# An unused room of 128 bytes a partition ahead of x, in a kernel of block attention and a squared-relu FFN

## The chip, the cores and the metric

One core of one Trainium2 chip. The metric is the device time of one execution in microseconds (us). The kernel before takes 895.19 us, the median of three runs (894.81 to 895.62).

## The reference

Attention inside chunks of 64 tokens, then a feed-forward network whose hidden values are `relu(h)` squared. All inputs and outputs are float32.

```python
def _attn_ref(q, k, v):                      # 8 batches, 8 heads, 576 tokens, 64 wide
    ...                                      # q_c, k_c, v_c: nine chunks of 64 tokens
    scores = scale * np.matmul(q_c, k_c.transpose(0, 1, 2, 4, 3))
    scores = scores - np.max(scores, axis=-1, keepdims=True)
    attn = np.exp(scores)
    attn = attn / (np.sum(attn, axis=-1, keepdims=True) + 1e-09)
    out = np.matmul(attn, v_c)
    ...
def _moe_ref(x, w_in, w_out):                # x 4608 x 512, w_in 512 x 2048, w_out 2048 x 512
    h = x @ w_in
    r = np.maximum(h, 0.0)
    g = r * r
    return (g @ w_out)
```

The weights come as 64-bit floats, and the kernel turns them into pairs of 32-bit floats itself.

## The kernel before, in words

The 4608 tokens are 36 pairs of chunks (128 tokens each), and four pairs make one of nine blocks of 512 tokens. For each block the attention writes x, transposed and as a sum of a high and a low part (tiles `xh`, `xl`, lines 338 to 342). The weights stand in SBUF all the time, converted once, each 128 x 512 piece as a high and a low part (`w`, line 176; sixteen rooms of 8192 bytes a partition, two pieces in each).

The FFN of a block has 16 steps f. A step has twelve matmuls of line 509 (`h` = weights x x: the stationary operand is a 128 x 128 slice of `w`, the moving operand 512 columns of `xh` or `xl`), then, two steps later, twelve of line 546 (`o` = g x weights: the stationary operand is a 128 x 128 slice of `gh` or `gl`, the moving operand 512 columns of `w`). Each product of two float32 is made of three: high by high, high by low, low by high. Between them ScalarE and VectorE make g of h (relu, square, high part, low part: lines 520, 524 or 526, 533, 536). On TensorE twelve of line 509 alternate with twelve of line 546, through the whole kernel; at four spots of a block this is broken by a group of 64 x 64 matmuls of the attention of the next block (lines 321 and 264). A planner (`Plan`, line 578) sets the order of the work of all engines from written costs; nothing in it knows addresses.

Tiles are taken from pools that lie one behind the other in each partition: `const` (line 84: `ident`, `warm`, and the sixteen rooms of the weights), `att` (line 85: the maxima `nm` and the sums `nz`, two rooms of 32 bytes each), `xp` (line 86: the tiles of x, 4096 bytes each, in which the results `outh` and `outl` stand as well), `gp` (line 87: `g`, `gh`, `gl`, 2048 bytes each, and one of the two rooms `a` of the weights' conversion), `wst` (line 94, the other `a`) and `nat` (line 120: the attention's own tiles). In the program as built, the rooms of the weights begin at addresses whose remainder to 256 is 160, and all tiles of `xp`, `gp`, `wst` and `nat` at addresses with the remainder 32. Slices inside the tiles of x, g and the weights that matmuls read begin at multiples of 512 bytes, so they keep these remainders.

So, in bytes to 256, a matmul of line 509 reads its moving operand at 32 and one of line 546 at 160. While a matmul runs, the weights of the next one are loaded. Inside a run of twelve of line 509 those are slices of `w` (160), inside one of line 546 slices of `gh` or `gl` (32): the two operands that are read at the same time stand 128 bytes apart to 256. At the change from one line to the other, the last matmul of line 509 (moving: x, 32) runs beside the load of `gh` (32), and the last one of line 546 (moving: `w`, 160) beside the load of `w` (160): there the two have the same remainder.

Of the kernel before, what the change touches and what calls it, by code (L numbers as in the profile page):

```python
# [11 lines left out]
F32 = mybir.dt.float32  # L12
# [10 lines left out]
def kernel(  # L23
# [24 lines left out]
    P = 128  # L48
# [34 lines left out]

    const = ctx.enter_context(tc.tile_pool(name="const", bufs=1))
    att = ctx.enter_context(tc.tile_pool(name="att", bufs=1))
    xp = ctx.enter_context(tc.tile_pool(name="xp", bufs=1))
    gp = ctx.enter_context(tc.tile_pool(name="gp", bufs=2))

# [1085 lines left out]
```

## Time and profile before

| | |
|---|---|
| median of three runs | 895.19 us |
| the profiled execution | 895.07 us |
| its span, from the first to the last instruction | 893.3 us |
| TensorE matmuls, busy | 876.3 us (98%) |
| TensorE weight loads, busy | 700.8 us (78%) |
| VectorE, busy | 410.4 us (46%) |
| ScalarE, busy | 341.8 us (38%) |
| GpSimd, busy | 35.2 us (4%) |
| mean granted clock of TensorE | 0.994 |

The times below are microseconds from the start of the span, in that one execution. PE is TensorE's matmuls, PEld its weight loads, DVE VectorE, ACT ScalarE, POOL GpSimd, SP the queue that issues transfers. The duration of one matmul (some 0.39 us) is longer than its distance to the next start (some 0.23 us), since matmuls are pipelined; what counts for the time is the distance of the starts.

### The profile page before, as it was taken

How to read it: one execution, taken by the hardware profiler on the slowest of the kernel's cores; microseconds unless marked ns; L12 is line 12 of the kernel's file. 1: busy time of each engine (PE TensorE's matmuls, PEld its weight loads, DVE VectorE, ACT ScalarE, POOL GpSimd, SP SyncE). 2: the span in 40 equal slices, each digit the busy share in tenths (PEclk: the TensorE clock that was granted, in tenths of full speed). 3: DMA queues.
4: the chain of work that ended last, by engine and by line, in shares of the span. 5: the costliest groups of instructions: out<-in, count | busy, mean ns of one | idle time of the engine just before them, and what ended most of it. 6: DMA issues, size and time to landing. Idle time of an engine off the chain costs nothing.

```text
span 893.3 us, 15034 instructions
## 1 busy us (share of the span) xinstructions
PE 876.3 (98%) x5890; PEld 700.8 (78%) x5890; DVE 410.4 (46%) x646; ACT 341.8 (38%) x568; POOL 35.2 (4%) x38
## 2 busy tenths in 40 slices
PE   6899999999999999999999999999999999999998
PEld 5676777887788888788888888888788887888886
DVE  5998984344444454444444443344434444322111
ACT  4889763332333333323333333223333333323222
POOL 1000000000000000000000000000000000000000
PEclk9899999999999999999999999999999999999999
DMA  9899133232422233222322232223222420001001
GB/s 218 216 293 282 31 84 98 55 74 60 107 60 59 59 85 82 59 55 52 100 55 48 58 102 57 56 57 101 59 61 61 106 48 24 25 1 48 1 1 47
DMA packets 214150, 70.21 MB, mean 79 GB/s; under 512 B 181312, under 2 KB 203840, under 8 KB 214080
## 3 DMA queue, kind: packets, MB, share of 16 engines
q1 hardware_dynamic: 211968, 68.73, 31.8%
q8 instruction: 46, 0.75, 0.3%
q10 hardware_dynamic: 2112, 0.52, 0.3%
q14 instruction: 24, 0.20, 0.1%
HBM read 52.43 MB, written 16.78 MB: 77 GB/s over the span
## 4 chain that ended last, share of the span: by engine, by line
PE 90%; DMA 5%; SPq 3%; DVE 1%; issue 0%; ACT 0%; ACTq 0%
PE o L546 43%; PE h L509 43%; DMA raw<-in_moe_w_out_dram 4%; PE at L321 2%; PE at L264 1%; SPq L222 1%; SPq L136 1%; SPq L230 1%; DMA qk_raw<-in_q_dram 0%; DVE w L189 0%; DMA vd<-in_v_dram 0%; PE qk L387 0%; PE xt L472 0%; SPq L138 0%; DVE raw L154 0%
## 5 line engine op out<-in xcount | busy, mean ns | idle before, releaser
L509 PE MATMUL h<-xh,w 128*128 128x512 f32 x1152 | 394.1, 398 | 1.3 <-DVE w L189 0.8
L546 PE MATMUL o<-w,gh 128*128 128x512 f32 x1152 | 361.9, 395 | 0.0
L509 PEld LDWEIGHTS h<-xh,w 128*128 128x128 f32 x1152 | 216.1, 188 | 54.7 <-DVE w L189 2.0
L546 PEld LDWEIGHTS o<-w,gh 128*128 128x128 f32 x1152 | 215.8, 188 | 51.1
L536 DVE TENSOR_TENSOR gl<-g,gh 128x512 fp32r<-128x512 f32 x144 | 117.5, 816 | 263.8 <-ACT gh L533 263.6
L546 PE MATMUL o<-w,gl 128*128 128x512 f32 x576 | 227.2, 394 | 0.0
L509 PE MATMUL h<-xl,w 128*128 128x512 f32 x576 | 227.0, 394 | 0.0
L520 ACT ACTIVATE g<-h 128x512 f32<-128x512 f32 x144 | 86.4, 600 | 255.6 <-PE h L509 207.2
L533 ACT CAST gh<-g 128x512 fp32r<-128x512 f32 x144 | 89.4, 621 | 184.8 <-PE o L546 184.6
L546 PEld LDWEIGHTS o<-w,gl 128*128 128x128 f32 x576 | 108.1, 188 | 25.9
L509 PEld LDWEIGHTS h<-xl,w 128*128 128x128 f32 x576 | 108.4, 188 | 24.1
L524 DVE TENSOR_TENSOR g<-g 128x512 f32<-128x512 f32 x64 | 44.3, 692 | 100.2 <-ACT g L520 100.0
L291 POOL TENSOR_TENSOR e<-e,z 128x512 f32<-128x512 f32 x28 | 30.3, 1083 | 719.5 <-DVE z L288 357.9
L526 ACT ACTIVATE g<-g 128x512 f32<-128x512 f32 x80 | 50.6, 632 | 2.4
L334 ACT CAST xh<-at 128x256 fp32r<-128x256 f32 x54 | 20.1, 373 | 72.8 <-PE at L264 52.3
L270 DVE TENSOR_REDUCE m<-at 128x8 f32<-128x512 f32 x27 | 18.7, 692 | 47.4 <-ACT xh L334 47.4
L253 DVE STREAM_TRANSPOSE turn<-raw 128x512 f32<-128x512 f32 x56 | 36.9, 690 | 0.1
L276 DVE TENSOR_TENSOR e<-at,m 128x512 f32<-128x512 f32 x27 | 18.6, 689 | 9.2 <-ACT xh L334 9.2
L321 PEld LDWEIGHTS at<-p,vd 64*64 64x64 f32 x864 | 15.1, 134 | 9.9 <-issue 9.5
L154 DVE TENSOR_SCALAR raw<-raw 128x1024 uint16<-128x1024 uint16 x16 | 21.5, 1388 | 1.3 <-ACT raw L150 1.3
L150 ACT ACTIVATE raw<-raw 128x1024 int32<-128x1024 uint32 x16 | 18.5, 1156 | 8.3 <-DMA raw<-in_moe_w_out_dram 5.8
L336 DVE TENSOR_TENSOR xl<-at,xh 128x256 fp32r<-128x256 f32 x54 | 20.4, 392 | 2.6 <-ACT xh L334 2.6
(67 smaller groups left out, 364.7 us busy)
## 6 DMA issues: line engine op xcount, KB each, us to landing
vd<-in_v_dram SPq DMA_DIRECT2D x144, 64.0 KB, 2.7
raw<-in_moe_w_in_dram SPq DMA_DIRECT2D x16, 512.0 KB, 6.5
raw<-in_moe_w_out_dram SPq DMA_DIRECT2D x16, 512.0 KB, 7.4
raw<-in_q_dram SPq DMA_DIRECT2D x224, 32.0 KB, 2.2
raw<-in_k_dram SPq DMA_DIRECT2D x224, 32.0 KB, 2.2
scr<-t SPq DMA_DIRECT2D x28, 256.0 KB, 2.3
p<-scr SPq DMA_DIRECT2D x112, 64.0 KB, 2.0
out_dram<-outh SPq DMA_DIRECT2D x18, 256.0 KB, 2.3
```

Of the source, the lines that this page charges most:

```text
L154: nc.vector.tensor_scalar(half[:, :, :, 1], half[:, :, :, 3], 0x8000, 0x4000, op0=ALU.bitwise_and, op1=ALU.bitwise_or)
L253: nc.vector.transpose(t.rearrange("p h i -> p (h i)"), self.raw[n].rearrange("p h a d -> p (h a d)"))
L291: nc.gpsimd.tensor_tensor(self.e, self.e, self.z.broadcast_to([P, HH, 2, CH]), op=ALU.mult)
L321: nc.tensor.matmul(self.xt[d, s, g, c].rearrange("p (b i) -> p b i", b=IH), vd[slot_of(self.u)][r, 2 * g + a, c], self.p[r, a, :, g, c], s ...
L336: nc.vector.tensor_tensor(x_of("l", b, s)[dst], src, xh.bitcast(F32)[dst], op=ALU.subtract)
L509: nc.tensor.matmul(self.h[:, :self.n], a[:, c], bb[:, c % HP, :self.n], start=c == 0 and i == 0, stop=c == NCC - 1 and i == 2,)
L520: nc.scalar.activation(self.g, self.h[:, :self.n], AF.Relu)
L524: nc.vector.tensor_tensor(self.g, self.g, self.g, op=ALU.mult)
L526: nc.scalar.activation(self.g, self.g, AF.Square)
L533: nc.scalar.copy(self.gh[:, :self.n], self.g)
L536: nc.vector.tensor_tensor(self.gl[:, :self.n], self.g, self.gh.bitcast(F32)[:, :self.n], op=ALU.subtract)
L546: nc.tensor.matmul(acc[b, j], a[:, j * P:(j + 1) * P], bb, start=f == 0 and i == 0, stop=f == NF - 1 and i == 2,)
```

## The change

One tile more in the pool `att`, ahead of all others of that pool: 2 x 16 float32, 128 bytes a partition. No instruction writes or reads it.

```diff
     att = ctx.enter_context(tc.tile_pool(name="att", bufs=1))
+    att.tile([P, 2, 16], F32, name="rest")
     xp = ctx.enter_context(tc.tile_pool(name="xp", bufs=1))
```

With it, everything that lies behind it, `nm` and `nz` and the pools `xp`, `gp`, `wst` and `nat`, moves by 128 bytes. `ident` and the weights stay. The remainder to 256 of x, g and the attention's tiles becomes 160, that of the weights. The remainders to 128 stay all as they were.

## Rows read from the trace of the kernel before

**Rows 1.** The page: engines' busy time (share) xinstructions; TensorE's clock in 40 slices
```profile
PE 876.3 (98%) x5890; PEld 700.8 (78%) x5890; DVE 410.4 (46%) x646; ACT 341.8 (38%) x568; POOL 35.2 (4%) x38
PEclk9899999999999999999999999999999999999999
```
**Rows 2.** Stages: stretch, length, busy time (count) by engine, clock, DMA share, GB/s
```profile
20.00:60.00 40.00, 35.37 (x297) 27.73 (x298) 37.89 (x54) 32.39 (x48) 2.09 (x2) 0.89 0.89 241
60.00:100.00 40.00, 37.43 (x251) 28.43 (x250) 37.58 (x49) 33.62 (x46) 0.00 (x0) 1.00 0.76 210
...
300.00:400.00 100.00, 100.00 (x665) 80.31 (x664) 43.04 (x70) 31.88 (x56) 4.48 (x5) 1.00 0.31 70
...
870.00:893.30 23.30, 19.27 (x84) 15.29 (x82) 2.77 (x4) 7.08 (x12) 0.00 (x0) 0.98 0.12 45
```
**Rows 3.** The same view, 100 to 870 us: line 509 alone, then line 546 alone
```profile
100.00:870.00 770.00, 395.70 (x1572) 292.81 (x1572) 1.00 0.26 60
...
100.00:870.00 770.00, 385.26 (x1565) 293.64 (x1564) 1.00 0.26 60
```
**Rows 4.** The chain that ended last: start, length, what; 437 to 457 us
```profile
437.63 2.80 PE o L546 x12
440.42 2.80 PE h L509 x12
443.22 2.80 PE o L546 x12
446.02 2.80 PE h L509 x12
...
454.41 2.80 PE o L546 x12
```
**Rows 5.** The same view, 800 to 879 us: first and last of 29 runs
```profile
800.19 2.78 PE h L509 x12
...
878.12 2.78 PE h L509 x12
```
**Rows 6.** Timeline, TensorE, the last 36 matmuls: start, length, instruction; first and last
```profile
880.75 0.62 PE L546 MATMUL o<-w,gh 128*128 128x512 f32 x2
...
888.88 0.39 PE L546 MATMUL o<-w,gl 128*128 128x512 f32 x1
```
**Rows 7.** Groups by line, windows around single matmuls, 442.59 to 443.69 us: busy, mean ns
```profile
L509 PE MATMUL h<-xl,w 128*128 128x512 f32 x1 | 0.4, 398 | 0.0
L509 PE MATMUL h<-xh,w 128*128 128x512 f32 x1 | 0.4, 390 | 0.0
L546 PE MATMUL o<-w,gh 128*128 128x512 f32 x1 | 0.4, 395 | 0.0
L546 PE MATMUL o<-w,gh 128*128 128x512 f32 x1 | 0.4, 392 | 0.0
L546 PE MATMUL o<-w,gl 128*128 128x512 f32 x1 | 0.4, 398 | 0.0
```
**Rows 8.** The same view: the matmul of 420.86 us and the weight load beside it
```profile
L546 PE MATMUL o<-w,gh 128*128 128x512 f32 x1 | 0.4, 404 | 0.0
...
L546 PEld LDWEIGHTS o<-w,gh 128*128 128x128 f32 x1 | 0.2, 192 | 0.0
```
**Rows 9.** Groups by line, the whole span: two-input subtractions of VectorE; weight loads
```profile
L189 DVE TENSOR_TENSOR w<-a,w 128x1024 fp32r<-128x1024 f32 x16 | 19.8, 1240 | 3.9 <-ACT w L178 3.9
L524 DVE TENSOR_TENSOR g<-g 128x512 f32<-128x512 f32 x64 | 44.3, 692 | 100.2 <-ACT g L520 100.0
L509 PEld LDWEIGHTS h<-xh,w 128*128 128x128 f32 x1152 | 216.1, 188 | 54.7 <-DVE w L189 2.0 <-ACT w L178 1.0
```
**Rows 10.** Transfers: line, xcount, KB each, us from issue to landing
```profile
p<-scr SPq DMA_DIRECT2D x112, 64.0 KB, 2.0
out_dram<-outh SPq DMA_DIRECT2D x18, 256.0 KB, 2.3
```

## The prediction

> **What bounds the kernel now.** I read the engines' table of the page first, then the stages, then the chain of waits, and last single matmuls. The table shows TensorE's matmuls busy for 98% of the span, while no other engine comes to half of it [rows 1]; the reader is to see one engine that has no idle time to give. The stages show where this holds. From 20 to 100 us TensorE is busy for 35.4 of 40 and 37.4 of 40 us, and VectorE, which converts the weights, for 37.9 and 37.6 of 40: there VectorE, ScalarE and the transfers of the weights set the pace. From 100 us on TensorE is busy all the time, at full granted clock, and VectorE for 43 of 100 us, ScalarE for 32 [rows 2]. So from 100 us to the end the time is the number of TensorE's matmuls times the distance between their starts, plus the attention's groups, and no wait ends late enough to matter.
>
> That number: 1572 matmuls of line 509 and 1565 of line 546 between 100 and 870 us [rows 3] and 84 after it [rows 2], together some 3220. The distance is not one number. In the chain of waits twelve matmuls in a row take 2.80 us in one part of a block and 2.78 us in another [rows 4, 5]. By the starts, the first kind has (454.41 - 437.63) / 72 = 233.1 ns a matmul, the second (878.12 - 800.19) / 336 = 231.9 ns. Each kind lasts until an attention group breaks the stream, and it runs on over changes of line, block and operand. The 84 matmuls at the end include 36 of line 546 in a row, without a change of line between them: their starts are (888.88 - 880.75) / 35 = 232.3 ns apart [rows 6].
>
> **What TensorE waits for in those 232 ns.** Nothing that the waits show: the weights' load of 188 ns [rows 9] begins with the matmul before and is over in time. But the durations of single matmuls are not all alike. In the first kind they alternate between 398 and 392 ns. In the second most lie between 390 and 396, and now and then one takes 404 ns, and then the weight load that runs beside it takes 192 ns in place of 188 [rows 8]. I read this as two streams out of the same memory, the moving operand and the next weights, which now and then meet and delay each other. Where they meet must depend on where both begin. That is the only thing that the change touches, so the question is whether the remainder to 256 bytes counts.
>
> The kernel before holds both cases. Inside a run the two streams stand 128 bytes apart to 256; at the change from one line to the other they have the same remainder for one matmul. Rows 7 show such a change. After the 398 of a matmul of line 509, 392 would follow; the last of line 509, beside the load of `gh`, has 390. Then 395 comes in place of 398, and from there 392 and 398 alternate again [rows 7]. Waits are not the cause as far as I can see: the third matmul of line 546 is fed by a load that also waits for a semaphore (`gl`), and around it durations are the usual 392 and 398 [rows 7]. So the address counts: a pair at equal remainder and its follower take 390 + 395 in place of 392 + 398, 5 ns less. The starts say the same of the other kind: a run of twelve with one change of line takes 231.9 x 12, without one 232.3 x 12 [rows 5, 6], 0.4 x 12 = 5 ns less for one change, with some 3 ns of uncertainty from the view's 10 ns steps.
>
> **The change part by part.**
>
> *TensorE's streams.* After it, every matmul stands beside a load at the same remainder, not one in twelve. If the 5 ns were a property of each such pair, all 3220 matmuls would save 5 ns: 16.1 us. If only the first of the two is its own effect (392 to 390) and the follower's 3 ns are an echo that the next pair writes over, they would save 2 ns: 6.4 us. I take 3 ns, between the two and nearer to the lower, since effects of neighbours will not simply add: 3220 x 3 ns = 9.7 us. All of it lies on the path that sets the end, as TensorE has no idle time there [rows 2]. What is late next: ScalarE and VectorE have more than half of their time free in those stages, so nothing takes the gain back.
>
> *The first 100 us.* TensorE waits there for converted weights, so I count nothing for it. The conversion itself has one instruction whose two inputs change their distance: the subtraction of line 189 reads `a` (moved) and `w` (not moved), 16 times 1240 ns for 1024 elements; line 524 reads one tile twice, at equal remainder, and takes 692 ns for 512 [rows 9]. Two of those are 1384 ns, so per element equal remainders are no faster, and the rows show no gain and no loss that I could name an address for. I take nothing; the difference of 144 ns in either direction times 16 would be 2.3 us, of which only what lies on VectorE's path before 100 us counts.
>
> *Transfers.* Tiles that transfers write or read move by 128 bytes too. Each is off the path but for the last store, 2.3 us to landing [rows 10]; another transfer with smaller pieces lands in 2.0, so 0.3 us either way bounds this, and I take nothing.
>
> *Instructions and waits.* None is added, and no tile gets another neighbour to wait for. GpSimd, ScalarE and the attention's tiles move together, so their distances stay.
>
> The sum: the profiled execution's 895.07 us (span 893.3 and 1.8 around it) less 9.7 is 885.4; the median of the runs lies 0.1 above that execution, so 885.5.
>
> **The rivals.**
>
> *No effect (0.25).* Two streams have to share a certain amount of reading whatever their start, and a limit of the whole cycle may be the same though each matmul's share differs. For it: the two kinds of stream differ in their pattern and yet only by 233.1 to 231.9 ns. Against it: rows 7. If the changed kernel only falls into the one kind or the other throughout, it takes 3220 times -0.8 to +0.4 ns against their middle of some 232.7: 892.5 to 896.4. The change may also not do what it says: a tile that nobody uses may get no room (I give that 0.03 of the 0.25); then the time is that of before, 895.2.
>
> [...]
>
> *Slower (0.22).* The mechanism is the same, with the other sign. A load begins with the matmul before. With equal remainders both streams would begin at the same place, and the meeting that now comes late or seldom would come at once, in each matmul. The rows at the change of line show single pairs that come out of a stream at the other distance; they do not show what a stream settles into that is at equal remainder throughout. If it settles at the long half of the first kind (398 in place of a mean of 395), it costs 3220 x 3 ns = 9.7 us: 904.8. If it settled at the 404 of rows 8, 29 us; I hold that for unlikely, since that one comes once in several matmuls now. The point from which it decides: matmuls inside a run above 396 ns in the mean.
>
> **How the numbers follow.** The forecast, faster by 2 to 5 ns a matmul or somewhat more, has 0.53: 885.5 us, own range 876 to 892. No effect has 0.25, slower 0.22. A measurement of this kernel can tell about 0.2% from no change, 1.8 us. For 8 in 10 the range has to take in no effect and half of the slower case: 876 to 904. Below 876 it would take more than 6 ns a matmul, which no pair of rows 7 shows; above 904 the long matmul throughout.
>
> **What would show it right or wrong.** In the profile after, right: twelve matmuls in the chain take less than 2.78 us, 2.75 to 2.76, in all blocks and on both lines alike, and the durations inside a run are those of a change of line now (390, 395) or lower, with no 404. The change of line itself is no longer to be seen in the durations, as the distance is the same there. Stages before 100 us and VectorE's durations stay. Wrong: 2.78 and 2.80 as before with the same 392 and 398 inside a run, which would mean that rows 7 show the change of tile or of the bank and not the address; or 2.83 and more, the slower case. If the time falls and the matmuls' distance doesn't, the first 100 us were the cause and my reading of TensorE was beside the point.

## The result, and the profile after

The changed kernel takes 875.64 us (875.26 to 875.75), the kernel before 895.40 in the same comparison: a ratio of 0.978, with a 95% interval of 0.976 to 0.979. It is faster by 2.2%, which is just outside the range on record (876 to 904): the sign and the place were right, the gain forecast was half of the true one.

The instructions are the same (15034 in both spans), and no engine but TensorE changes its busy time by more than a few tenths of a microsecond: VectorE has 410.1 us, ScalarE 341.8, GpSimd 35.1. TensorE's matmuls fall from 876.3 to 858.4 us (against [rows 1]). From the page of the changed kernel, engines' busy time:

```profile
PE 858.4 (98%) x5890; PEld 702.0 (80%) x5890; DVE 410.1 (47%) x646; ACT 341.8 (39%) x568; POOL 35.1 (4%) x38
```

The stages, columns as in [rows 2]. From 100 us on TensorE is as busy as before; before 100 us it still waits at times:

```profile
20.00:60.00 40.00, 35.62 (x291) 28.16 (x292) 36.75 (x53) 31.41 (x46) 2.08 (x2) 0.83 0.89 246
60.00:100.00 40.00, 38.48 (x261) 30.39 (x261) 39.55 (x53) 34.99 (x49) 0.00 (x0) 1.00 0.72 204
...
300.00:400.00 100.00, 100.00 (x676) 82.21 (x675) 41.18 (x68) 33.09 (x58) 4.18 (x4) 1.00 0.30 68
```

The chain of waits (start, length, what) answers [rows 4, 5]. Around 437 us, where the kernel before had twelve matmuls in 2.80 us, and in the last block, where it had 2.78:

```profile
437.14 2.72 PE h L510 x12
439.87 2.72 PE o L547 x12
442.58 2.72 PE h L510 x12
...
801.89 2.72 PE o L547 x12
...
859.01 2.72 PE h L510 x12
861.73 8.17 PE o L547 x36
```

There is one kind of stream now, with the same distance on both lines: (859.01 - 801.89) / (21 x 12) = 226.7 ns a matmul, in place of 233.1 and 231.9. Single durations, by the view of one line (smallest, median, largest), first of the kernel before, then of the changed one:

```profile
L509 PE MATMUL h<-xh,w x1152: 387/395/504, 32.4 to 880.5; 128*128 128x512 f32 x192
```
```profile
L510 PE MATMUL h<-xh,w x1152: 387/389/776, 33.9 to 861.3; 128*128 128x512 f32 x192
```

And the windows around matmuls of 442 us, which answer [rows 7]: the last of line 547, then two of line 510.

```profile
L547 PE MATMUL o<-w,gl 128*128 128x512 f32 x1 | 0.4, 389 | 0.0
...
L510 PE MATMUL h<-xh,w 128*128 128x512 f32 x1 | 0.4, 389 | 0.0
...
L510 PE MATMUL h<-xl,w 128*128 128x512 f32 x1 | 0.4, 389 | 0.0
```

Inside the full runs of twelve 398 and 392 are gone from 170 us on, where 389 stands in their place, and a change of line can't be told from the inside of a run. (The duration of a record goes with the distance to the next start: 389 ns stand with 227, 396 with 232, 404 with 241. The two are one piece of evidence, and the distance is the one that makes the time.)

Where the 19.4 us of the spans came from: the same run of twelve stands at 117.13 us in the chain of before and at 115.87 in that of after, and the last run of 36 at 880.91 and 861.73:

```profile
117.13 2.80 PE o L546 x12
...
880.91 8.38 PE o L546 x36
```
```profile
115.87 2.72 PE o L547 x12
...
861.73 8.17 PE o L547 x36
```

So 1.3 us were gained up to there, 17.9 us between the two, and 0.2 in the last run. The middle part holds 3120 matmuls of the two lines: 5.7 ns each.

### The profile page after: what moved, and what is told of

It is laid out like the page before. It is cut to its first block, busy times and chain, and to the rows that moved or that the text cites. A ratio compares the mean times of both kernels' runs of the same rounds, so it can differ in the third digit from the quotient of the medians.

```text
span 873.9 us, 15034 instructions
## 1 busy us (share of the span) xinstructions
PE 858.4 (98%) x5890; PEld 702.0 (80%) x5890; DVE 410.1 (47%) x646; ACT 341.8 (39%) x568; POOL 35.1 (4%) x38
## 4 chain that ended last, share of the span: by engine, by line
PE 88%; DMA 5%; DVE 3%; SPq 2%; ACT 1%; issue 1%; ACTq 0%; DVEq 0%
PE o L547 42%; PE h L510 42%; DMA raw<-in_moe_w_out_dram 3%; PE at L322 2%; PE at L265 1%; DMA raw<-in_moe_w_in_dram 1%; SPq L231 1%; DMA qk_raw<-in_q_dram 1%; DVE raw L155 1%; SPq L223 1%; DMA qk_raw<-in_k_dram 1%; DVE w L190 0%; SPq L137 0%; DVE gl L537 0%; ACT raw L151 0%
## 5 line engine op out<-in xcount | busy, mean ns | idle before, releaser
L510 PE MATMUL h<-xh,w 128*128 128x512 f32 x1152 | 388.0, 393 | 0.4 <-DVE w L190 0.4
L547 PE MATMUL o<-w,gh 128*128 128x512 f32 x1152 | 355.7, 390 | 0.0
L510 PE MATMUL h<-xl,w 128*128 128x512 f32 x576 | 224.5, 390 | 0.0
L547 PE MATMUL o<-w,gl 128*128 128x512 f32 x576 | 224.2, 389 | 0.0
L190 DVE TENSOR_TENSOR w<-a,w 128x1024 fp32r<-128x1024 f32 x16 | 19.8, 1235 | 1.6 <-ACT w L179 1.6
```

Of the source, the lines that this page charges most:

```text
L510: nc.tensor.matmul(self.h[:, :self.n], a[:, c], bb[:, c % HP, :self.n], start=c == 0 and i == 0, stop=c == NCC - 1 and i == 2,)
L547: nc.tensor.matmul(acc[b, j], a[:, j * P:(j + 1) * P], bb, start=f == 0 and i == 0, stop=f == NF - 1 and i == 2,)
```

## The experiments

Two theories stood against each other. *Distance*: what counts is how far, in bytes to 256, the moving operand of a matmul stands from the weights that are loaded beside it. *Place*: what counts is the remainder of x and g themselves, or of the other tiles that moved (the attention's, VectorE's). All runs but those at 16 and 8 bytes, and the repetition, are edits of the kernel before, by rooms that nobody uses at the front of pools. The distance below is the moving operand's remainder less that of the loaded one.

### All tiles moved together

```diff
     const = ctx.enter_context(tc.tile_pool(name="const", bufs=1))
+    const.tile([P, 32], F32, name="room_c")
```

> A room of 128 bytes ahead of the first tile of the pool const, none in att. All tiles move by 128 bytes together: to 256 the weights stand at 32, x and g at 160, so the moving operand and the weights loaded beside it stay 128 bytes apart, but x, g and the attention's tiles have the addresses of the changed kernel. Theory of the distance (what counts is the two streams' distance to 256): as before, 895 us, twelve matmuls in 2.78 to 2.80 us. Rival, the address of x and g themselves (or of the attention's tiles): as after the change, 876 us, 2.72 us for twelve.

Measured: 895.37 us against 894.55, ratio 1.0005 (0.999 to 1.002). x, g and all tiles behind them have the very remainders of the changed kernel, and nothing is gained. Place falls.

### All moved, and x once more

```diff
+    const.tile([P, 32], F32, name="room_c")
...
+    att.tile([P, 32], F32, name="room_a")
```

> A room of 128 bytes at the front of const and another at the front of att: to 256 the weights, x and g all stand at 32. x, g and the attention's tiles have the remainder that they had before the change, and the weights have another. Theory of the distance: 876 us, 2.72 us for twelve matmuls, durations of 389 ns all alike. Rival, the address of x and g themselves: 895 us, 2.78 to 2.80 us.

Measured, in two executions: 879.53 us, ratio 0.982 (0.978 to 0.986), with x and g at 32 as in the kernel before. Twelve matmuls in 2.72 us on both lines, by the chain of waits:

```profile
800.57 2.72 PE o L548 x12
803.29 2.72 PE h L511 x12
```

Distance holds. The 4 us over the changed kernel are not in the matmuls' distance: the run of twelve that stands at 115.87 us there stands at 119.98 here, and the last run of 36 at 865.85 in place of 861.73, so all of it came before.

```profile
119.98 2.72 PE o L548 x12
...
865.85 8.17 PE o L548 x36
```

In the stages TensorE was busy for 7.79 us between 70 and 80 us here, with the transfers of the weights at work (325 GB/s), where the changed kernel has 9.61 (290 GB/s). Whether the weights' addresses have a part in that was not tried; the kernel with all tiles moved, with the same addresses of the weights, shows no loss (895.37 us against 894.55, within the noise).

### x alone, g alone

With both rooms x alone moves (the second room brings g and all behind it back to 32); with the second room only, g moves, and with it the tiles behind it.

```diff
     att = ctx.enter_context(tc.tile_pool(name="att", bufs=1))
+    att.tile([P, 32], F32, name="room_a")
...
     gp = ctx.enter_context(tc.tile_pool(name="gp", bufs=2))
+    gp.tile([P, 32], F32, name="room_g", bufs=1)
```

> The room of 128 bytes at the front of att and another at the front of the pool gp: x moves to 160 to 256, the remainder of the weights; g, the attention's tiles and the conversion's rooms stand at 32 as before. Line 509 (x beside weights) is at equal remainder, line 546 (weights beside g) 128 bytes apart. Theory of the distance: runs of twelve of line 509 take 2.72 to 2.74 us, those of line 546 2.78 to 2.80, half the gain, 885 to 886 us. Rival, that one part alone brings all of it (x as the operand that matters): 876 us and 2.72 us on both lines; rival, that the attention's tiles or VectorE's rooms are what matters: 895 us.

> The room of 128 bytes at the front of gp alone: g, the conversion's rooms and the attention's tiles move to 160, x stays at 32. Line 546 is at equal remainder, line 509 128 bytes apart. Theory of the distance: runs of line 546 take 2.72 to 2.74 us, those of line 509 2.78 to 2.80; 885 to 886 us. Rival, that the tiles behind gp (attention, VectorE's rooms) bring the gain: 876 us with 2.72 us on both lines cannot come of that, but a time below 885 with line 509 as before and the first 100 us shorter would show a share of theirs.

Measured: x alone 891.28 us (ratio 0.996, 0.9945 to 0.998), g alone 887.57 us (0.992, 0.990 to 0.994). In each the line at equal remainder is the faster one, as the distance theory has it, but the gains are 3.3 and 7.0 us, together 10 and not 20; half of the whole gain was expected of each. With g alone nothing below 885 us shows a share of the attention's tiles or of VectorE's rooms. The chains say where the rest is, x alone first:

```profile
438.76 2.76 PE h L511 x12
441.52 2.80 PE o L548 x12
```
```profile
437.29 2.79 PE h L510 x12
440.08 2.73 PE o L547 x12
```

With x alone, a run of line 511 at equal remainder takes 2.76 us, not 2.72. Its starts, from the timeline, at the first, eighth and twelfth matmul:

```profile
438.60 0.40 PE L511 MATMUL h<-xh,w 128*128 128x512 f32 x1
...
440.22 0.39 PE L511 MATMUL h<-xl,w 128*128 128x512 f32 x1
...
441.13 0.40 PE L511 MATMUL h<-xh,w 128*128 128x512 f32 x1
```

The first seven distances are (440.22 - 438.60) / 7 = 231 ns, the last four 0.91 / 4 = 227. So here a stream that comes from the other distance needs seven matmuls to settle, and of a run of twelve five are left by then. With g alone three matmuls are enough: in the last run of 36 they take 392, 395 and 393 ns, and from the fourth to the end of the run the distance is (881.45 - 874.20) / 32 = 226.6 ns:

```profile
873.50 0.39 PE L547 MATMUL o<-w,gh 128*128 128x512 f32 x1
...
874.20 0.39 PE L547 MATMUL o<-w,gh 128*128 128x512 f32 x1
...
881.45 0.39 PE L547 MATMUL o<-w,gl 128*128 128x512 f32 x1
```

The two kernels also tell which operands count. With x alone, the last matmul of line 511 has its moving operand at 160 and its own weights at 160, and beside it `gh` at 32 is loaded. It takes 396 ns; the one ahead of it, with the same two operands but `w` at 160 loaded beside it, has 389. It is so in all 99 full runs of line 511 after 120 us that stand between two of line 548, while in the changed kernel the same place has 389 in all. (The first row is the window around the matmul of 440.90 us, the second that of 441.13.)

```profile
L511 PE MATMUL h<-xl,w 128*128 128x512 f32 x1 | 0.4, 389 | 0.0
...
L511 PE MATMUL h<-xh,w 128*128 128x512 f32 x1 | 0.4, 396 | 0.0
```

With g alone it is the other way round: the last matmul of line 547 has its own weights and the next ones at 160, and keeps 389; the first of line 510 behind it, with x at 32 beside `w` at 160, has 395 (both in the window around 442.79 us).

```profile
L510 PE MATMUL h<-xh,w 128*128 128x512 f32 x1 | 0.4, 395 | 0.0
L547 PE MATMUL o<-w,gl 128*128 128x512 f32 x1 | 0.4, 389 | 0.0
```

So in these two kernels a matmul's duration goes with the next weights and not with its own: 389 ns where the next ones have the remainder of its moving operand, 396 and 395 where they stand 128 bytes from it.

### The distance in steps

```diff
+    att.tile([P, n], F32, name="room_a")   # n = 64, 16, 24, 40, 56: 256, 64, 96, 160, 224 bytes
```

> A room of 256 bytes in place of 128 at the front of att: x, g and the attention's tiles move, but to 256 they stand at 32 again, 128 from the weights. Theory of the distance to 256: as before, 895 us, 2.78 to 2.80 us for twelve matmuls, the same durations as before. Rival, that the distance to 512 bytes counts (128 before, 256 after, 384 here), or that any other place of x would have brought the gain: a time between 870 and 890 us.

> A room of 64 bytes at the front of att: x and g stand at 96 to 256, 64 below the weights' 160. If the cost grows with the distance on the circle of 256 bytes (0: 226.7 ns a matmul, 128: 232.7 ns), 64 gives some 229.7 ns and 885.5 us. Rival, that only the same 32 bytes (or less) count as equal: 895 us. Rival, that equal is a special point with worse neighbours: above 897 us.

> A room of 96 bytes at the front of att: x and g stand at 128 to 256, 32 below the weights. If the cost grows with the distance on the circle: 228 ns a matmul, 880 us. Rival, that only equal remainders help: 895 us. If another place than the equal one is the best, this or the room of 160 bytes should show it with less than 875 us. This also moves x and g from 32 to 0 to 32... to 128, a multiple of 128, and so tells whether such an address is worth something by itself.

> A room of 160 bytes at the front of att: x and g stand at 192 to 256, 32 above the weights. By the distance alone as with 32 below: 228 ns a matmul, 880 us. But line 509 and line 546 swap the roles of the two operands, so a difference of sign must show between the lines: if the moving operand ahead is better, line 509 is faster than line 546 here, and the other way round with x and g 32 below.

> A room of 224 bytes at the front of att: x and g stand at 0 to 256. Line 509 has its moving operand 96 bytes above the loaded one (to 256), line 546 96 below. Found so far, moving operand above the loaded one: 0: 226.7 ns a matmul, +32: 233.2, +64: 229.4 to 230, 128: 232.9, -64: 233.4, -32: 233.3. If cost is a smooth function of the signed distance, +96 lies between 229.5 and 233 and -96 between 233 and 233.4: 889 to 895 us, line 509 the faster one. If every multiple of 64 is a good place for one sign and the rest is bad: both lines 233, 895 us.

The steps below 32 bytes are edits of the changed kernel. The tiles of x, `gh` and `gl` are made 256 bytes longer, so that their neighbours keep their remainders, and what they hold stands 16 or 8 bytes further in:

```diff
-            xt[m, b, hq] = xp.tile([P, HP, XB[b % 2] * P], F32R, name=name, tag=name[:-1] + str(b % 2))
+            room = xp.tile([P, HP * XB[b % 2] * P + 64], F32R, name=name, tag=name[:-1] + str(b % 2))
+            xt[m, b, hq] = room[:, 4:4 + HP * XB[b % 2] * P].rearrange("p (a n) -> p a n", a=HP)
...
-                gp.tile([P, MAXB * P], F32R, name=f"g{m}{s}", tag=f"g{m}", bufs=GBUFS) for m in "hl"
+                gp.tile([P, MAXB * P + 64], F32R, name=f"g{m}{s}", tag=f"g{m}", bufs=GBUFS)[:, 4:4 + MAXB * P]
+                for m in "hl"
```

> The changed kernel with the tiles of x, gh and gl 256 bytes longer and their contents 16 bytes further in: line 509's moving operand 16 bytes above the loaded one to 256, line 546's 16 below. The loads begin 2 to 4 ns after the matmul; if the best place is where the two streams begin at the same place at the same time, one sign should be better than equal and the other worse: one line below 226.7 ns, the other above. [...]

> The same with 8 bytes in place of 16. If there is a better place than equal remainders on one side of it, one line is below 226.7 ns a matmul here or at 16 bytes; if equal is a sharp point, both lines are above it and the time lies between 876 and 895 us.

Measured, with twelve matmuls of each line from the chain of waits between 800 and 865 us, and the last run of 36, which is all of o. Each ratio is to the kernel before in the same comparison, 894.93 us for the four steps from 256 to 160 and 895.60 for the last three:

| room, or shift | distance of h's matmuls | twelve, us | distance of o's matmuls | twelve, us | last 36, us | time, us | ratio (95% interval) |
|---|---|---|---|---|---|---|---|
| none (before) | 128 | 2.78 | 128 | 2.78 | 8.38 | 895.40 | 1 |
| 128 (after) | 0 | 2.72 | 0 | 2.72 | 8.17 | 875.64 | 0.978 (0.976 to 0.979) |
| 256 | 128 | 2.78 | 128 | 2.78 | 8.38 | 895.55 | 1.001 (0.999 to 1.002) |
| 64 | -64 | 2.80 | +64 | 2.76 to 2.79 | 8.27 | 892.46 | 0.997 (0.996 to 0.998) |
| 96 | -32 | 2.80 | +32 | 2.80 | 8.42 | 896.34 | 1.001 (1.000 to 1.002) |
| 160 | +32 | 2.80 | -32 | 2.80 | 8.42 | 896.26 | 1.002 (1.001 to 1.003) |
| 224 | +96 | 2.80 to 2.81 | -96 | 2.79 to 2.81 | 8.44 | 895.58 | 1.000 (0.999 to 1.001) |
| 128, and 16 in | +16 | 2.77 to 2.78 | -16 | 2.74 to 2.79 | 8.19 | 890.73 | 0.994 (0.992 to 0.995) |
| 128, and 8 in | +8 | 2.80 to 2.82 | -8 | 2.77 | 8.32 | 892.58 | 0.997 (0.996 to 0.998) |

Two of the views behind it, 16 bytes in and then 8 bytes in:

```profile
800.07 2.74 PE o L549 x12
802.81 2.77 PE h L511 x12
805.58 2.79 PE o L549 x12
...
877.63 8.19 PE o L549 x36
```
```profile
799.93 2.77 PE o L549 x12
802.70 2.82 PE h L511 x12
...
878.05 8.32 PE o L549 x36
```

The room of 256 bytes moves x, g and all tiles behind them and gives the kernel before back, so no moving as such helps. By itself it does not tell 256 bytes from 512. In the program as built the distance to 512 is 128 on line 509 and -128 on line 546 in the kernel before, and this room only swaps the two; in the changed kernel it is 256, and no kernel has it at 0. The run with 16 bytes in does tell, by the fourth and the last matmul of its last run of 36:

```profile
878.17 0.39 PE L549 MATMUL o<-w,gh 128*128 128x512 f32 x1
...
885.42 0.39 PE L549 MATMUL o<-w,gl 128*128 128x512 f32 x1
```

Its longer tiles put the two rooms of `gh`, and those of `gl`, 256 bytes apart to 512. This run of 36 uses one, then the other, then the first again, and the distance of its starts is (885.42 - 878.17) / 32 = 226.6 ns throughout. There 256 bytes more or less make no difference, so the distance counts to 256 bytes (or a part of it).

My guess of a cost that grows with the distance was wrong: 32 bytes off, on either side, the whole gain is gone. At 32 bytes the durations go by the sign and not by the line: with 96 bytes those of h (at -32) alternate between 395 and 396 ns and those of o (at +32) repeat 393, 396, 394, 397; with 160 bytes the two lines have changed places.

The times and the runs of twelve suggest that equal remainders are a sharp point, with the gain mostly gone at 8 and 16 bytes. The last run of 36 shows it otherwise. In these kernels the lines stand on opposite sides of the weights, so the stream changes its distance at every change of line, and twelve matmuls may not be enough to settle. In the last run, with one distance throughout, o's matmuls at -16 come down to the 226.6 ns of equal remainders after three matmuls, as they did with g alone. At -8 they do not: 8.32 us, 230.5 ns. At +64 it is 8.27 us, some 229 ns once settled; at 32 on either side 8.42, some 233. Earlier in the kernel at -16, some of o's runs of twelve come down (2.74 us) and others do not (2.79); what decides between them no run shows, nor what h would settle into at +8 or +16, as it has no run of 36. Of the places tried, equal remainders are the only one where both lines take 2.72 us, and none is better.

### The changed kernel again

> The changed kernel beside the other runs of this call. The room at the front of const and att (all tiles at 32) took 879.5 us with the same 226.9 ns a matmul; if its 4 us more are of the addresses, this takes 875 to 876 us here; if they are of the chip and of when the weights land in the first 100 us, up to 880.

Measured, in two executions: 876.38 us, beside 895.6 for the kernel before on the same chip (0.978, 0.974 to 0.982). The gain repeats. What made the 4 us of the kernel with both rooms stays open, as that one ran on another chip.

## Why the prediction was wrong in its size

- **What bounds the kernel**: right. From 100 us on, time is matmuls times their distance, and the 5.7 ns saved on each arrive at the end whole.
- **That the address counts, read from the change of line**: right. All moved together (895.4) and all moved with x once more (879.5) show the distance and not the place; the 396 ns with x alone and the 389 and 395 with g alone show that it is the weights loaded beside the matmul.
- **3 ns a matmul**: this is the step that failed. It measured 5.7 ns in the middle part: 17.9 us over 3120 matmuls, where 3220 x 3 ns = 9.7 us were forecast. I read one pair at equal remainder in the kernel before, 390 + 395 in place of 398 + 392, as a sample of a stream at equal remainder. It is only the first step into it: the runs with x alone and g alone take three to seven matmuls to come down to 389 ns each, and with g alone the first two take 392 and 395, near to the 390 and 395 that I read. In the kernel before, the one pair at each change of line never had a second behind it. What it could show was that the address counts and not by how much; even the upper bound that I made of it, 5 ns, was no bound, as nothing in the rows showed the settled state. My rival *Slower* says that single pairs do not show what a stream settles into; I held that against the sign of the forecast and not against its size.
- **Slower, by the long matmul in each**: it did not come. Inside the full runs 398 is gone from 170 us on, and the streams settle at the short end, 389 ns. A stream at 404 throughout is ruled out with it.
- **No effect**: ruled out at this kernel's distances. The same instructions take 226.7 ns a matmul at equal remainders and 231.9 or 233.1 at 128 bytes, by nothing but 128 bytes of address, and 875.64 us lies below the 892.5 that this rival allowed.
- **First 100 us, transfers, VectorE**: nearly right. 1.3 us came before 117 us, where I counted nothing; how much of it is the 308 matmuls that run there, and how much waiting, was not separated. Without these 1.3 us the time would have been 876.9 us: that it fell outside the range hangs on them, that the size was wrong does not. VectorE's line 189 (now 190) changed from 1240 to 1235 ns, which the bound of 144 ns covers:

```profile
L190 DVE TENSOR_TENSOR w<-a,w 128x1024 fp32r<-128x1024 f32 x16 | 19.8, 1235 | 1.6 <-ACT w L179 1.6
```

- **What would show it right**: I named 2.75 to 2.76 us for twelve, both lines alike, no sign of a change of line in the durations. Both lines are alike and the change of line is gone; the 2.72 us lie below what I named.

## What to carry to other kernels

This was tried on one kernel, with float32 operands of 512 columns. Here equal remainders to 256 bytes of the moving operand and the next stationary one gave 226.7 ns a matmul in place of 231.9 and 233.1, and an unused room of 128 bytes a partition ahead of a pool made them equal. Where TensorE is the bound and each matmul has a weight load beside it, that comparison is worth making in every stage; what it brings has to be measured there. A change at a boundary inside a trace can show that a cause exists, but where the effect needs several instructions to settle, its size has to be measured in a stream that is in that state throughout. Here three to seven matmuls passed until one settled. The same holds for a scan over addresses: where neighbouring runs stand at different distances, a short run shows the change between them and not the place (o at -16: 2.74 and 2.79 us for twelve, 226.6 ns a matmul once settled in the run of 36). In this kernel a small tile ahead of such operands moved the time by 2.2% without any instruction being different, so it is worth a look at the addresses before such a difference is put down to an edit itself.

## What the runs showed of the hardware that I had not expected

- The distance between matmuls of 512 float32 columns with a load of 128 columns beside each is 226.7 ns at equal remainders to 256 bytes, 233 ns at 32 bytes to either side, 231.9 or 233.1 at 128.
- Equal remainders are not alone: with the loaded weights 16 bytes above the moving operand the last run of 36 settles at the same 226.6 ns, with 8 bytes at 230.5.
- The sign counts: at 32 bytes each sign has its own pattern of durations, on either line (395 and 396 ns at -32; 393, 396, 394 and 397 at +32), with the same 2.80 us. At +64 (moving operand ahead) o has runs of 2.76 us, at -64 h has 2.80; there sign and line were not separated.
- With x or g alone moved, a stream needs three to seven matmuls to settle at equal remainders, and at -16 some runs of twelve do not. At 128 bytes two different patterns last for tens of microseconds each with the same instructions: in the kernel before 2.80 us for twelve from 437.63 us to 457.20, 2.78 from 800.19 to 880.91.
- The 64 x 64 matmuls of the attention (line 321 of the kernel before), whose two operands stand in one pool and move together, keep their 224 ns in the mean at every placement tried.

Why the distance to 256 bytes counts no run here tells.
